# Two decode layers on one core: 256 rows of the second layer's w2 on a few partitions, in small loads among the large ones

## The chip, the cores and the metric

The kernel runs on one core of one Trainium2 chip. The metric is the device time of one execution in microseconds; lower is better. Every number below is from one profiled execution of the kernel before, or from its timed runs.

## The reference

Two layers, each an attention block and a gated feed-forward block, both with the same weights and the same caches, for four tokens in fp32:

```python
x = A_x                                           # 4 x 1 x 512
for _ in range(2):
    x = x + A(layernorm(x), k_cache, v_cache, wq, wo)
    x = x + B(layernorm(x), w1, w3, w2)

def A(x, k_cache, v_cache, wq, wo):               # 32 query heads, 8 KV heads, 4096 keys, 128 wide
    p = softmax(q @ k.T * 128 ** -0.5)
    return (p @ v) @ wo

def B(x, w1, w3, w2):                             # w1, w3: 512 x 1792, w2: 1792 x 512
    return (silu(x @ w1) * (x @ w3)) @ w2
```

## The kernel before

All weights and both caches come from HBM once per layer, except what is kept from layer 0 to layer 1 (wq, most of wo, and K and V of one head group, `TURN`). One buffer, `arena`, holds 216 units of 256 floats in each of 128 partitions. A list, `plan`, says in which order pieces are loaded; `pump` goes through it and issues each piece with one DMA on SyncE's queue (SP, L163) as soon as `take` finds room, and the instructions that read a piece call `done`, which gives its room back. On the chip SP works through its list strictly in order. Each DMA has one of eight semaphores, in turn, so a DMA is not issued before the one eight places ahead of it has landed; it also waits until TensorE (PE) has read what lay at its place.

In a layer, for each of eight head groups, PE forms the scores (`scores`, L371, into `s_ps`), VectorE (DVE) and ScalarE (ACT) the exponents, and PE the weighted sum of V (`weigh`, L414, into `o_ps`). `project_o` (L438, L445) multiplies by wo. Then comes `feed_forward`. w1 and w3 each come in two parts, "a" (columns 0 to 255 of each quarter of the 1792) and "b" (the other 192). `product` (L478) multiplies by them, into `s_ps` and `o_ps`; `gate` (ACT, L486, and DVE, L487) and `join` (DVE, L491) make h of them, with four tokens times four quarters on the partitions that are used. PE transposes h by 128 columns at a time (L525, L538, L540) and `tiles` (DVE, L494) copies the result to `hT`, 14 tiles of 128 x 4, which `down` multiplies with the 14 tiles of w2. In layer 1 a tile of w2 takes four matmuls (L503), one for each 128 columns of the output, each to its own 32 rows of `x_ps`; a matmul of fp32 is two instructions in the trace. `busy` (L259) issues matmuls whose result nobody reads. After the last tile DVE copies `x_ps` to `p` (L596) and SP stores it (L597).

In layer 1 the last loads are, in this order: 4 MB, 2 MB and 2 MB of V, w1a and w3a (2 MB each), w1b and w3b (1.5 MB each), and w2 in six loads of 1, 1, 0.5, 0.5, 0.25 and 0.25 MB. The first K of layer 0 comes in two loads of 4 MB, and the last V of layer 0 (group `TURN`) in four, of 4, 2, 1 and 1 MB, followed by wo.

Of the kernel before, what the change touches and what calls it, by code (L numbers as in the profile page):

```python
# [9 lines left out]
AF = mybir.ActivationFunctionType  # L10
# [4 lines left out]
LAYERS = 2  # L15
REP = HQ // HKV
P = 128
# [6 lines left out]
FA = 2 * P  # L24
FB = FJ - FA
WT = 14
EPS = 1e-5
SCALE = DH ** -0.5

# [5 lines left out]


@with_exitstack
def tile_decode_layers(ctx: ExitStack, tc: tile.TileContext, x, kt, v, wq, wo, w1, w3, w2, out):
# [51 lines left out]
    def cache(which, layer, g, parts, skip=0):  # L90
        src = (kt if which == "k" else v)[g]
        r = 8 * skip
        for n in parts:
            at = KEPT + r if (which, layer, g) in (("v", 0, TURN), ("k", 1, TURN - 2)) else None
            load(src[:, r * KB:(r + n) * KB], 8, [(which, layer, g, r // 8 + j) for j in range(n // 8)], at)
            r += n

    def weights(name, src, layer, parts, per, at=None, first=0):
        r = 0
        for n in parts:  # L100
            load(src[:, r * KB:(r + n) * KB], per, [(name, layer, first + r // per + j) for j in range(n // per)],
                 None if at is None else at + r)
            r += n
# [1 line left out]
    order = [list(range(HKV)), list(reversed(range(HKV)))]  # L105
    load(wq[:, 0:8 * KB], 8, [("wq", 0, 0)], WQ)
    for n in range(HKV):
        cache("k", 0, n, (32, 32) if n == 0 else (64,))
        if n == 0:
            load(wq[:, 8 * KB:64 * KB], 8, [("wq", 0, g) for g in range(1, HKV)], WQ + 8)  # L110
        else:
            cache("v", 0, n - 1, (64,))
    cache("v", 0, TURN, (32, 16, 8, 8))
    weights("wo", wo, 0, (32, 16, 8, 4, 4), 4, WO)

    def piece(name, i, at):
# [39 lines left out]
    def pump():  # L156
        while state["next"] < len(plan):
            src, per, keys, at = plan[state["next"]]
            n = src.shape[-1] // KB
            a = take(n, at)  # L160
# [69 lines left out]
    hT = qT.rearrange("p h c -> p (h c)")[:, 0:WT * B].rearrange("p (m b) -> p m b", b=B)  # L230
    top = const.tile([P, 32], F32, name="top")
    nc.vector.memset(top, 0.0)

# [236 lines left out]
    def feed_forward(layer, mean):  # L470
        keep = layer < LAYERS - 1
        h = p[:, 0:FJ]

        def product(name, ps, lo, n, fill=keep, ks=range(KC)):
            for k in ks:
                w = loaded(name, layer, k)
                for j in range(4):
                    nc.tensor.matmul(ps[32 * j:32 * j + 32, lo:lo + n], x32[:, k, :], w[:, j * n:(j + 1) * n],  # L478
                                     start=(k == 0), stop=(k == KC - 1))
                done(name, layer, k)  # L480
                if fill:
                    busy()

        def gate(lo, n):
            a = h[:, lo:lo + n]
            nc.scalar.activation(a, s_ps[:, lo:lo + n], AF.Sigmoid, scale=rstd)  # L486
            nc.vector.scalar_tensor_tensor(a, s_ps[:, lo:lo + n], rstd, a, op0=ALU.mult, op1=ALU.mult)  # L487

        def join(lo, n):
            a = h[:, lo:lo + n]  # L490
            nc.vector.scalar_tensor_tensor(a, o_ps[:, lo:lo + n], rstd, a, op0=ALU.mult, op1=ALU.mult)  # L491

        def tiles(lo, n):
            nc.vector.tensor_copy(hT[:, 4 * lo:4 * lo + n, :], t_ps.rearrange("p i (j b) -> p (i j) b", j=4)[:, 4 * lo:4 * lo + n, 0:B])  # L494

        def down(i):
            ws = [loaded("w2", layer, 2 * i + n) for n in range(2)]
            if keep:
                pair(i, lambda m: hT[:, m, :], lambda n: ws[n], i == 0, i == WT // 2 - 1)
            else:  # L500
                for n in range(2):
                    for k in range(KC):
                        nc.tensor.matmul(x_ps[32 * k:32 * k + B, 0:P], hT[:, 2 * i + n, :],  # L503
                                         ws[n][:, k * P:(k + 1) * P], start=False, stop=(i == WT // 2 - 1 and n == 1))
            for n in range(2):
                done("w2", layer, 2 * i + n)
            if keep and i < WT // 2 - 1:
                busy()
            elif not keep and i in (1, 3):
                busy(3)  # L510
# [12 lines left out]
        nc.scalar.activation(spare, half, AF.Exp)  # L523
        for i in range(2):
            nc.tensor.transpose(t_ps[:, i, :], h[:, i * P:(i + 1) * P], ident)  # L525
# [6 lines left out]
        if layer == LAYERS - 1:  # L532
            nc.vector.tensor_tensor(xt, xc, mu.unsqueeze(1).broadcast_to([P, KC, B]), op=ALU.add)
            for k in range(KC):
                nc.tensor.matmul(x_ps[32 * k:32 * k + B, 0:P], xt[:, k, :], ident, start=True, stop=False)

        def tail_tiles():
            nc.tensor.transpose(t_ps[:, 2, :], h[:, FA:FA + P], ident)  # L538
# [3 lines left out]
            tiles(2, 6)  # L542

        for i in range(1 if keep else 0, WT // 2):
            if i == (4 if keep else 0):
                tail_tiles()
            down(i)

    def run(pieces):
        for _ in pieces:  # L550
# [86 lines left out]
```

## Time and profile before

| | |
|---|---|
| timed runs | 708.88, 708.69 and 706.84 us, median 708.69 |
| the profiled execution's own time | 706.78 us |
| its span, first to last instruction | 705.0 us |
| HBM read | 298.85 MB |
| PE busy | 400.1 us (57%) |
| DVE busy, ACT busy | 85.0 us (12%), 38.3 us (5%) |
| SP's DMA queue | 99.1% of the time of the 16 DMA engines |

The share of a DMA queue is the time that its packets took, over 16 engines times the span; 99.1% means that hardly any engine was ever without a packet. A DMA is cut into packets, one for each row here, and spread over several of the 16 engines; each engine ends its part with a packet of 4 bytes that counts the semaphore up. The engine times are unions of the instructions' times. The time of an execution is 1.8 us more than its span.

### The profile page before, as it was taken

The numbers are of one execution on the slowest core, as the hardware profiler recorded it, in microseconds if no ns is written. First come the engines' busy times: TensorE is split into PE (matmuls) and PEld (weight loads), VectorE is DVE, ScalarE is ACT, GpSimd is POOL, SyncE is SP. The second block draws the span as 40 slices with busy tenths as digits, with TensorE's granted clock in tenths as the row PEclk, the third lists the DMA queues.
The fourth block names the chain that finished last, engine by engine and source line by source line (L and its number), as shares of the span: only waits on it lengthen the run. The fifth ranks groups of instructions, "written<-read, shape, count | busy, mean of one in ns | idle before, by whom it ended". The sixth has DMA issues, their size and how long they took to land. (4 is left out here: it accounts for less than half of the span.)

```text
span 705.0 us, 6895 instructions
## 1 busy us (share of the span) xinstructions
PE 400.1 (57%) x3082; PEld 132.1 (19%) x3082; DVE 85.0 (12%) x290; ACT 38.3 (5%) x87; POOL 2.9 (0%) x10
## 2 busy tenths in 40 slices
PE   4555454546555553547677894365563545467666
PEld 2111011111111120112143231011120111122224
DVE  2001010101011010101111111020010101010111
ACT  0000000000000000002001000000000000000101
POOL 0000000000000000000000000000000000000000
PEclk9766777777677787768899997587697878788899
DMA  9999999999999999999999999999999999999996
GB/s 387 461 403 472 414 417 436 450 417 431 455 416 432 435 436 420 442 421 423 413 404 406 416 438 438 446 424 421 461 421 424 440 439 421 431 432 419 426 425 270
DMA packets 14003, 299.35 MB, mean 425 GB/s; under 512 B 1687, under 2 KB 1815, under 8 KB 6551
## 3 DMA queue, kind: packets, MB, share of 16 engines
q1 hardware_dynamic: 13840, 298.92, 99.1%
q8 instruction: 24, 0.39, 0.2%
q10 hardware_dynamic: 135, 0.01, 0.0%
q14 instruction: 4, 0.03, 0.0%
HBM read 298.85 MB, written 0.07 MB: 424 GB/s over the span
## 5 line engine op out<-in xcount | busy, mean ns | idle before, releaser
L414 PE MATMUL o_ps<-arena 128*32 128x512 f32 x1024 | 145.7, 718 | 150.8 <-DMA arena<-in_v 137.6
L371 PE MATMUL s_ps<-arena,qpad 128*32 128x512 f32 x1024 | 152.1, 749 | 82.5 <-DMA arena<-in_kt 82.5
L414 PEld LDWEIGHTS o_ps<-arena 128*32 128x32 f32 x1024 | 37.3, 129 | 257.3 <-issue 224.5
L371 PEld LDWEIGHTS s_ps<-arena,qpad 128*32 128x32 f32 x1024 | 39.5, 133 | 177.7 <-issue 165.6
L423 DVE SCALAR_TENSOR_TENSOR p<-o_ps,parts,p 128x512 f32<-128x512 f32 x16 | 12.0, 750 | 270.9 <-PE o_ps L414 270.9
L378 DVE TENSOR_REDUCE top<-s_ps 128x1 f32<-128x512 f32 x16 | 11.0, 690 | 194.0 <-PE s_ps L371 194.0
L315 PE MATMUL o_ps<-arena,xpad 128*32 128x512 f32 x112 | 16.2, 707 | 10.5 <-DMA arena<-in_wq 10.5
L421 ACT ACTIVATE p<-o_ps,parts 128x512 f32<-128x512 f32 x16 | 11.0, 687 | 192.5 <-PE o_ps L414 184.6
L445 PE MATMUL x_ps<-arena,oT 128*4 128x512 f32 x104 | 14.1, 653 | 9.1 <-DMA arena<-in_wo 5.6
L402 PE MATMUL t_ps<-ident,p 128*128 128x128 f32 x64 | 11.2, 302 | 13.5 <-ACT p L396 13.5
L425 PE MATMUL t_ps<-ident,p 128*128 128x128 f32 x64 | 10.5, 287 | 14.3 <-DVE p L423 14.2
L389 ACT ACTIVATE f<-d 128x1 f32<-128x1 f32 x16 | 3.2, 203 | 256.3 <-DVE d L387 256.3
L396 ACT ACTIVATE p<-s_ps,top 128x512 f32<-128x512 f32 x16 | 10.9, 684 | 75.9 <-PE t_ps L425 75.9
L425 PEld LDWEIGHTS t_ps<-ident,p 128*128 128x128 f32 x64 | 6.7, 141 | 29.6 <-DVE p L423 29.6
L403 DVE COPY arena<-t_ps 128x512 f32<-128x512 f32 x16 | 11.1, 691 | 9.6 <-PE t_ps L402 9.6
L259 PE MATMUL m_ps<-ident,rows 128*32 128x128 f32 x70 | 11.9, 273 | 0.0
L402 PEld LDWEIGHTS t_ps<-ident,p 128*128 128x128 f32 x64 | 7.1, 147 | 22.2 <-ACT p L396 19.2
L478 PE MATMUL o_ps<-arena,xpad 128*32 128x192 f32 (+1 forms) x128 | 8.1, 360 | 2.9 <-DMA arena<-in_w 2.8
L478 PE MATMUL s_ps<-arena,xpad 128*32 128x192 f32 (+1 forms) x128 | 7.9, 359 | 2.3 <-DMA arena<-in_w 2.1
L259 PEld LDWEIGHTS m_ps<-ident,rows 128*32 128x32 f32 x70 | 7.5, 110 | 3.5
L315 PEld LDWEIGHTS o_ps<-arena,xpad 128*32 128x32 f32 x112 | 3.7, 126 | 20.7 <-DMA arena<-in_wq 11.6
L320 DVE COPY p<-o_ps 128x256 f32<-128x256 f32 x2 | 0.8, 424 | 44.9 <-PE o_ps L315 44.9
(97 smaller groups left out, 139.9 us busy)
## 6 DMA issues: line engine op xcount, KB each, us to landing
arena<-in_kt SPq DMA_DIRECT2D x4, 4096.0 KB, 20.1
arena<-in_v SPq DMA_DIRECT2D x4, 4096.0 KB, 33.0
arena<-in_w SPq DMA_DIRECT2D x17, 512.0 KB, 10.1
arena<-in_kt SPq DMA_DIRECT2D x8, 1024.0 KB, 9.8
arena<-in_wq SPq DMA_DIRECT2D x1, 7168.0 KB, 39.5
arena<-in_v SPq DMA_DIRECT2D x3, 2048.0 KB, 36.8
arena<-in_wo SPq DMA_DIRECT2D x1, 4096.0 KB, 25.5
arena<-in_kt SPq DMA_DIRECT2D x8, 512.0 KB, 8.2
```

Of the source, the lines that this page charges most:

```text
L259: nc.tensor.matmul(m_ps[turn["m"] ^ 1][0:32, 384:512], rows, ident, start=True, stop=True)
L315: nc.tensor.matmul(ps[32 * k:32 * k + 32, :], xpad[:, k, lo:lo + 32], w[:, k, :], start=first, stop=last)
L371: nc.tensor.matmul(s_ps[32 * b:32 * b + 32, :], qpad[:, b, lo:lo + 32], k[:, j, :], start=(blk == 0), stop=(blk == NB - 1))
L378: nc.vector.tensor_reduce(top[:, 0:1], s_ps, axis=AX.X, op=ALU.max, negate=True)
L402: nc.tensor.transpose(t_ps[:, i, :], p[:, i * P:(i + 1) * P], ident)
L403: nc.vector.tensor_copy(pT.rearrange("p i r -> p (i r)"), t_ps.rearrange("p i r -> p (i r)"))
L414: nc.tensor.matmul(o_ps[32 * b:32 * b + 32, :], pT[:, i, 32 * b:32 * b + 32], w[:, b, :], start=(i == 0), stop=(i == NI - 1))
L421: nc.scalar.activation(p, o_ps, AF.Copy, scale=st["parts"][:, 0:1])
L423: nc.vector.scalar_tensor_tensor(p, o_ps, st["parts"][:, 1:2], p, op0=ALU.mult, op1=ALU.add)
L425: nc.tensor.transpose(t_ps[:, j, :], p[:, j * P:(j + 1) * P], ident)
L445: nc.tensor.matmul(x_ps[r:r + B, :], left(2 * i + n), w(n), start=first, stop=False)
L478: nc.tensor.matmul(ps[32 * j:32 * j + 32, lo:lo + n], x32[:, k, :], w[:, j * n:(j + 1) * n], start=(k == 0), stop=(k == KC - 1))
```

## The change

The last V of layer 0 comes in two loads of 4 MB in place of four, and the first K in one load of 8 MB in place of two. In layer 1, tiles 0 and 4 of w2 (rows 0 to 255 of the 1792) are no longer loaded as 128 partitions. They come as nine blocks: eight of 28 rows on partitions 0 to 27, and one of 32 rows on partitions 0 to 31. The eight blocks lie side by side, 16 KB in a partition, and come in four loads, each of every fourth partition (7 rows of 16 KB); the ninth is a load of 32 rows of 2 KB. These five loads (`aside`) stand ahead of w1a, w3a, w1b, w3b and the first large load of w2. The other 12 tiles come in loads of 0.75, 0.75, 0.5, 0.5, 0.25 and 0.25 MB. For the nine blocks h has to be transposed in pieces of 28 (and 32) columns, by nine matmuls with the identity, and each block takes four matmuls with as many contraction rows (`few`). The residual's matmuls (`xt`) and some of the blocks' now stand ahead of w3b's product, `gate` of part b stands behind the transposes, and an exponential on one column that layer 1 had there (for the ACT table) is gone, as is `busy(4)` ahead of it; `busy(3)` twice is now `busy(2)` twice.

```diff
-        cache("k", 0, n, (32, 32) if n == 0 else (64,))
+        cache("k", 0, n, (64,))
...
-    cache("v", 0, TURN, (32, 16, 8, 8))
+    cache("v", 0, TURN, (32, 32))
...
+    side = iter([(w2s[i::4], slice(i, FEW, 4), 0) for i in range(4)] + [(w2b, slice(0, 32), 16)])
+    def aside():
+        plan.append((*next(side), None))
+    aside()
     for part, per, at in (("a", 4, 0), ("b", 3, 16)):
         for name, w in (("w1", w1), ("w3", w3)):
             weights(name + part, w[:, at * KB:(at + 4 * per) * KB], 1, (4 * per,), per)
-    weights("w2", w2, 1, (8, 8, 4, 4, 2, 2), 2)
+            aside()
+    for m, parts in ((1, (6,)), (5, (6,)), (8, (4, 4, 2, 2))):
+        weights("w2", w2[:, 2 * m * KB:], 1, parts, 2, None, m)
...
+                nc.sync.dma_start(arena[per, (a + keys) * KB:(a + keys + n) * KB], src)
...
+        def columns(rows, m, w, last=False):
+            for k in range(KC):
+                nc.tensor.matmul(x_ps[32 * k:32 * k + B, 0:P], hT[rows, m, :], w[rows, k * P:(k + 1) * P],
+                                 start=False, stop=last)
+        def few(lo, hi):
+            for u in range(lo, hi):
+                at = (where["few"] + 2 * u) * KB
+                columns(slice(0, FEW if u < 8 else 32), WT + u, arena[:, at:at + 2 * KB])
...
-        if not keep:
-            busy(4)
-        gate(FA, FB)
-        nc.scalar.activation(spare, half, AF.Exp)
+        if keep:
+            gate(FA, FB)
+            nc.scalar.activation(spare, half, AF.Exp)
         for i in range(2):
             nc.tensor.transpose(t_ps[:, i, :], h[:, i * P:(i + 1) * P], ident)
+        if not keep:
+            for u in range(9):
+                n = FEW if u < 8 else 32
+                nc.tensor.matmul(t_ps[0:n, 2, B * u:B * u + B], h[0:32, FEW * u:FEW * u + n], ident[0:32, 0:B],
+                                 start=True, stop=True)
         tiles(0, 8)
+        if not keep:
+            nc.vector.tensor_copy(hT[0:32, WT:WT + 9, :], t_ps[0:32, 2, 0:9 * B].rearrange("p (u b) -> p u b", b=B))
+            gate(FA, FB)
+            nc.vector.tensor_tensor(xt, xc, mu.unsqueeze(1).broadcast_to([P, KC, B]), op=ALU.add)
+            for k in range(KC):
+                nc.tensor.matmul(x_ps[32 * k:32 * k + B, 0:P], xt[:, k, :], ident, start=True, stop=False)
+            few(0, 4)
         product("w3b", o_ps, FA, FB, ks=range(0, 2))
...
         product("w3b", o_ps, FA, FB, ks=range(2, KC))
         join(FA, FB)
...
+        few(4, 7)
+        tail_tiles()
+        few(7, 9)
+        for m in (1, 2, 3, 5, 6, 7, *range(8, WT)):
+            columns(slice(0, P), m, loaded("w2", layer, m), m == WT - 1)
+            done("w2", layer, m)
+            if m in (3, 7):
+                busy(2)
```

The order of the instructions, first on SP at the end of layer 1. A row is line, operation, tile written and tensor read, and partitions times elements; `x2` is two of them in a row. Before:

```order
L163 DMA arena<-in_v 128x4096 x2
L163 DMA arena<-in_w 128x4096 x2
L163 DMA arena<-in_w 128x3072 x2
L163 DMA arena<-in_w 128x2048 x2
L163 DMA arena<-in_w 128x1024 x2
L163 DMA arena<-in_w 128x512 x2
L597 DMA out<-p 128x128
```

and now:

```order
L184 DMA arena<-in_v 128x4096 x2
L178 DMA arena<-in_w2s 7x4096
L184 DMA arena<-in_w 128x4096
L178 DMA arena<-in_w2s 7x4096
L184 DMA arena<-in_w 128x4096
L178 DMA arena<-in_w2s 7x4096
L184 DMA arena<-in_w 128x3072
L178 DMA arena<-in_w2s 7x4096
L184 DMA arena<-in_w 128x3072
L178 DMA arena<-in_w2b 32x512
L184 DMA arena<-in_w 128x1536 x2
```

Each small load now stands ahead of a large one, and the first two loads of w2 are a quarter smaller; the last four are as before.

On PE, from w1b's product (the 16 matmuls into `s_ps`) to the end. Before:

```order
L478 MATMUL s_ps<-arena,xpad 32x192 x16
L259 MATMUL m_ps_120<-ident,rows 32x128 x4
L525 MATMUL t_ps<-ident,p 128x128 x2
L478 MATMUL o_ps<-arena,xpad 32x192 x16
L535 MATMUL x_ps<-ident,xt 4x128 x4
L538 MATMUL t_ps<-ident,p 128x128
L540 MATMUL t_ps<-ident,p 64x64 x2
L503 MATMUL x_ps<-arena,qT 4x128 x16
L259 MATMUL m_ps_120<-ident,rows 32x128 x3
L503 MATMUL x_ps<-arena,qT 4x128 x16
L259 MATMUL m_ps_120<-ident,rows 32x128 x3
L503 MATMUL x_ps<-arena,qT 4x128 x24
```

and now (`qT` is the memory in which `hT` lies):

```order
L499 MATMUL s_ps<-arena,xpad 32x192 x16
L548 MATMUL t_ps<-ident,p 128x128 x2
L552 MATMUL t_ps<-ident,p 28x4 x8
L552 MATMUL t_ps<-ident,p 32x4
L560 MATMUL x_ps<-ident,xt 4x128 x4
L528 MATMUL x_ps<-arena,qT 4x128 x16
L499 MATMUL o_ps<-arena,xpad 32x192 x16
L528 MATMUL x_ps<-arena,qT 4x128 x12
L569 MATMUL t_ps<-ident,p 128x128
L571 MATMUL t_ps<-ident,p 64x64 x2
L528 MATMUL x_ps<-arena,qT 4x128 x20
L280 MATMUL m_ps_119<-ident,rows 32x128 x2
```

Behind the last row come 12 matmuls into `x_ps`, two more of `busy` and 24 into `x_ps`. Between w1b's product and w3b's stand 31 matmuls where there were six.

More of the change, by code (lines that the diff above doesn't have):

```diff
@@ L26 @@
 WT = 14
+FEW = 28
 EPS = 1e-5
@@ L37, in tile_decode_layers @@
 @with_exitstack
-def tile_decode_layers(ctx: ExitStack, tc: tile.TileContext, x, kt, v, wq, wo, w1, w3, w2, out):
+def tile_decode_layers(ctx: ExitStack, tc: tile.TileContext, x, kt, v, wq, wo, w1, w3, w2, w2s, w2b, out):
     nc = tc.nc
@@ L159, in pump @@
             n = src.shape[-1] // KB
+            if isinstance(per, slice):
+                where.setdefault("few", None if "few" in where else take(18))
+                a = where["few"]
+                if a is None:
+                    del where["few"]
+                    return
+                nc.sync.dma_start(arena[per, (a + keys) * KB:(a + keys + n) * KB], src)
+                state["next"] += 1
+                continue
             a = take(n, at)
@@ L229, in tile_decode_layers @@
     oT = const.tile([P, HKV, REP, B], F32, name="oT")
-    hT = qT.rearrange("p h c -> p (h c)")[:, 0:WT * B].rearrange("p (m b) -> p m b", b=B)
+    hT = qT.rearrange("p h c -> p (h c)")[:, 0:(WT + 9) * B].rearrange("p (m b) -> p m b", b=B)
     top = const.tile([P, 32], F32, name="top")
@@ L493, in tiles @@
         def tiles(lo, n):
-            nc.vector.tensor_copy(hT[:, 4 * lo:4 * lo + n, :], t_ps.rearrange("p i (j b) -> p (i j) b", j=4)[:, 4 * lo:4 * lo + n, 0:B])
+            slots = t_ps.rearrange("p i (j b) -> p (i j) b", j=4)
+            nc.vector.tensor_copy(hT[:, lo:lo + n, :], slots[:, lo:lo + n, 0:B])
         def down(i):
             ws = [loaded("w2", layer, 2 * i + n) for n in range(2)]
[L498 to L504, printed above, removed]
+            pair(i, lambda m: hT[:, m, :], lambda n: ws[n], i == 0, i == WT // 2 - 1)
             for n in range(2):
                 done("w2", layer, 2 * i + n)
-            if keep and i < WT // 2 - 1:
+            if i < WT // 2 - 1:
                 busy()
-            elif not keep and i in (1, 3):
-                busy(3)
+        def columns(rows, m, w, last=False):
[6 more added lines that the diff above has]
+                columns(slice(0, FEW if u < 8 else 32), WT + u, arena[:, at:at + 2 * KB])
         sq = squares()
@@ L531, in feed_forward @@
         join(FA, FB)
[L532 to L535, printed above, removed]
         def tail_tiles():
@@ L541, in tail_tiles @@
                                  start=True, stop=True)
[L542 to L547, printed above, removed]
+            tiles(8, 6)
+        if keep:
+            for i in range(1, WT // 2):
+                if i == 4:
+                    tail_tiles()
+                down(i)
+            return
+        few(4, 7)
+        tail_tiles()
+        few(7, 9)
[4 more added lines that the diff above has]
+                busy(2)
     def run(pieces):
@@ L626 @@
         "w2": lay(np.concatenate([full, rest], axis=1)).reshape(P, WT * D),
+        "w2s": lay(w2j[0, :8 * FEW].reshape(8, FEW, D).transpose(1, 0, 2)).reshape(FEW, 8 * D),
+        "w2b": lay(w2j[0, 8 * FEW:2 * P]),
     }
```

## The prediction

> **What bounds the kernel now.** I read the page first, for what is busy, then the chain that ended last, then the end in windows of half a microsecond. The page, with the 40 slices of the DMA engines' busy share and the queues:
>
> ```profile
> span 705.0 us, 6895 instructions
> DMA  9999999999999999999999999999999999999996
> q1 hardware_dynamic: 13840, 298.92, 99.1%
> q8 instruction: 24, 0.39, 0.2%
> q10 hardware_dynamic: 135, 0.01, 0.0%
> ```
>
> The loads' queue fills 16 engines for 99.1% of the span, and only the last slice is below nine tenths. So time is won or lost only through bytes, their rate, their spread over the engines, or the work behind the last byte. q8 fetches instructions: 24 packets of 16 KB take 0.2% x 16 x 705 = 22.6 us of engine time, 0.94 us each, on whichever engines serve it. The end of the chain (start, length, what):
>
> ```profile
> 643.63 41.49 DMA arena<-in_w
> ...
> 685.19 16.14 DMA arena<-in_w
> 701.33 0.04 issue
> 701.37 0.45 PE x_ps L503 x8
> ...
> 701.84 0.29 DVE p L596
> ```
>
> The last load lands at 701.33 us, one tile's matmuls and a copy follow. Everything that ends the kernel is on this line: landing, then 0.49 us to the end of PE's work, then 3.2 us for the copy and the store to 705.0. Now the end by windows; the last two columns are the share of 16 DMA engines and GB/s:
>
> ```profile
> 696.00:697.00 1.00, 1.00 (x30) 0.95 (x18) 0.00 (x0) 0.00 (x0) 0.00 (x0) 1.00 0.88 344
> 697.00:697.50 0.50, 0.22 (x3) 0.00 (x0) 0.00 (x0) 0.00 (x0) 0.00 (x0) 1.00 0.70 279
> 697.50:698.00 0.50, 0.45 (x18) 0.44 (x22) 0.00 (x0) 0.00 (x0) 0.00 (x0) 1.00 0.68 270
> 698.00:698.50 0.50, 0.50 (x25) 0.49 (x14) 0.00 (x0) 0.00 (x0) 0.00 (x0) 1.00 0.52 209
> 698.50:699.00 0.50, 0.50 (x13) 0.50 (x12) 0.00 (x0) 0.00 (x0) 0.00 (x0) 1.00 0.49 197
> 699.00:699.50 0.50, 0.50 (x19) 0.34 (x10) 0.00 (x0) 0.00 (x0) 0.00 (x0) 1.00 0.42 168
> 700.00:700.50 0.50, 0.42 (x16) 0.33 (x16) 0.00 (x0) 0.00 (x0) 0.00 (x0) 1.00 0.43 164
> ```
>
> 0.70 of 16 is 11 engines, 0.49 is 8, 0.42 is 7: nine engines end between 696.5 and 699.5, and seven go on alone to about 701. Each engine got the same bytes of the loads, so something else held the seven up; the fetches of q8, by their size, are the likely one, though no view names the engine of a packet.
>
> **The loads, part by part.** How many engines a load uses follows from the packet counts above. 96 loads and stores of 128 rows at 128 + 16 packets, and one of 8 rows at 8 + 8, make 13840; the ACT queue's 120 rows make 135 = 120 + 15. So 128, 8 and 120 rows ran on 16, 8 and 15 engines, each the largest number up to 16 that divides the rows. Then 7 rows run on seven engines and 32 on 16. The rate of one engine, from the stretch of large loads and from the middle of the tail:
>
> ```profile
> 200.00:300.00 100.00, 53.18 (x370) 16.21 (x366) 10.80 (x33) 4.80 (x11) 0.00 (x0) 0.76 1.00 434
> 320.00:340.00 20.00, 14.53 (x110) 4.57 (x110) 3.47 (x9) 3.30 (x6) 0.00 (x0) 0.91 0.99 419
> 360.00:370.00 10.00, 7.41 (x93) 3.78 (x93) 1.37 (x6) 0.59 (x2) 0.56 (x1) 1.00 1.03 400
> 692.00:693.00 1.00, 0.45 (x12) 0.39 (x16) 0.00 (x0) 0.44 (x2) 0.00 (x0) 1.00 1.02 414
> ```
>
> 434 / 16 = 27.1 GB/s for long rows, 414 / 16 = 25.9 at the end. Every engine loses two tiles of w2, 32 KB, and gains 4 KB of the ninth block: 28 KB / 25.9 = 1.11 us less. Seven engines get four rows of 16 KB more: 64 KB / 27.1 = 2.42, so 1.31 us more in all. Whether the landing moves down or up hangs on which seven. If they are among the nine early ones, the late seven land 1.11 us earlier, and the loaded ones at the latest at 699.5 + 1.3 = 700.8. If they are the late seven, the landing moves up by 1.31. No row tells engines apart. [...]
>
> Layer 0's last V: 4 MB in rows of 16 and 8 KB become rows of 32 KB. Between 419 GB/s (the stretch in which they land) and 434 lie 4.19 MB / 419 - 4.19 MB / 434 = 0.35 us; nothing is the other end. I take 0.2 us for all engines. The first K's rows go from 32 to 64 KB: nothing to see.
>
> What the two joined loads cost: PE can start only when all has landed. For V:
>
> ```profile
> 334.34 3.64 PE L414 MATMUL o_ps<-arena 128*32 128x512 f32 x32 [1.21 <-ACT p L421]
> 345.17 6.82 PE L445 MATMUL x_ps<-arena,oT 128*4 128x512 f32 x48 [5.59 <-DMA arena<-in_wo]
> ```
>
> The second half's 32 instructions end at 337.98 and PE then waits 5.59 us for wo. The four last blocks would start at most 3.64 us later; the wait for wo covers that. I cost it at nothing; without that cover it would be up to 3.6 us on all that follows. The first K behaves alike: half of its scores come later, while loads issued long before keep coming. SP's five more loads, against three fewer before, shift who waits for which of the eight semaphores: the last load of w2 will wait for the fourth small one instead of w3a. Behind that one stand 4.3 MB up to the last load, 10 us at 419 GB/s, more than the spread of the engines, so none runs dry.
>
> [...]
>
> **PE behind w1b, part by part.** The added matmuls lie beside loads only as long as PE keeps ahead of the landings. The rows of the tail:
>
> ```profile
> 682.45 1.11 PE L297 MATMUL m_ps<-rows,p 128*128 128x4 f32 x8 [0.56 <-DVE p L290]
> 684.06 1.45 PEld L478 LDWEIGHTS s_ps<-arena,xpad 128*32 128x32 f32 x32 [0.36 <-DVE xpad L301]
> 688.95 1.51 PE L478 MATMUL s_ps<-arena,xpad 128*32 128x192 f32 x32 [0.56 <-DMA arena<-in_w]
> 690.97 0.42 DVE L487 SCALAR_TENSOR_TENSOR p<-s_ps,rstd,p 128x192 f32<-128x192 f32 x1 [1.93 <-ACT p L486]
> 691.22 0.44 PE L525 MATMUL t_ps<-ident,p 128*128 128x128 f32 x2
> 691.69 0.19 DVE L494 COPY qT<-t_ps 128x32 f32<-128x32 f32 x1 [0.31 <-PE t_ps L525]
> 692.55 1.51 PE L478 MATMUL o_ps<-arena,xpad 128*32 128x192 f32 x32 [0.89 <-DMA arena<-in_w]
> 694.12 0.42 DVE L491 SCALAR_TENSOR_TENSOR p<-o_ps,rstd,p 128x192 f32<-128x192 f32 x1 [2.24 <-PE o_ps L478]
> 694.46 0.17 DVE L533 TENSOR_TENSOR xt<-xpad,mu 128x16 f32<-128x16 f32 x1
> 694.68 0.40 PE L535 MATMUL x_ps<-ident,xt 128*4 128x128 f32 x8 [0.62 <-DVE xt L533]
> 695.01 0.33 PE L538 MATMUL t_ps<-ident,p 128*128 128x128 f32 x1
> 695.53 1.06 PE L503 MATMUL x_ps<-arena,qT 128*4 128x128 f32 x32
> 696.40 0.82 PE L259 MATMUL m_ps<-ident,rows 128*32 128x128 f32 x6
> ```
>
> Now PE waits for loads (0.89 us before w3b, for instance). The new order, from w1b's start at 688.95 - 0.2 = 688.75: product 1.51, two transposes 0.44, to 690.7. Nine small transposes are 18 instructions; they load 28 columns of weights and stream four. No row shows that: 1.45 / 32 = 0.045 us each (weights of 32 columns) is one end, 0.8 us in all, and 1.11 / 8 = 0.139 (128 columns, four streamed) the other, 2.5 us. The first is nearer, since loading sets the pace in both; with some for four streamed columns I take 0.06, 1.1 us: 691.8. DVE, in its order: copy 0.19, gate 0.42, xt 0.17, with 0.1 between them: 692.7. PE: xt's matmuls 0.33 to the next, four blocks at the price of four tiles 1.06, w3b 1.51: 695.6. join 0.48 with its start, beside three blocks (0.80): 696.4. Tail transposes 0.52 (695.01 to 695.53), two blocks 0.53, three tiles 0.80, `busy(2)` 0.45 (two thirds of 0.82, part of it overlapped), three tiles 0.80, `busy(2)` 0.45, six tiles 1.59: 701.5. With the ends of the small transposes: 701.2 and 702.9.
>
> **The sum.** The end of PE's work was 701.82. By the loads it would be 701.33 - 1.11 - 0.2 + 0.49 = 700.5, up to 701.1 if a loaded engine is last. By PE it is 701.5. The later one holds: 0.3 us less, 706.78 - 0.3 = 706.5 us against this execution's own time. That execution was 1.9 us below the median of the runs (708.69; one run at 706.84, two at 708.7 to 708.9), a spread as large as all I argue about; 0.3 below the median is 708.4. I state the middle of the two, 707.4 us.
>
> **The rivals.** (a) PE keeps up, and the loads set the end: shorter transposes, or blocks that run faster with 28 rows. Then 1.3 us less, 705.5 or 707.4 by the median. For it speaks that my PE chain is a sum of separate rows; against it that it holds hardly a wait to shorten. (b) Slower: the seven engines of the small loads are the late seven. It decides as soon as one loaded engine ends later than 700.0: landing 701.33 + 1.31 - 0.2 = 702.4, 1.1 us more, 707.9 or 709.8. [...] (c) Slower: the small transposes cost their upper end and PE ends at 702.9, 1.1 us more. (d) The load of 7 rows runs on one engine: 28 rows of 16 KB / 27.1 are 16.9 us on it, less 1.1; even the earliest engine, done at 696.5, would then end near 712, 11 us more, 718. The packet counts speak against. (e) The joined V or K opens a gap, or the runs' two levels change their mix: 2 us either way, 704.7 or 710.7.
>
> **How the numbers follow.** Forecast 0.40, (a) 0.27, (b) 0.11, (c) 0.08, (d) 0.02, (e) 0.12, evenly both ways. A measurement here can hardly tell 0.3%, 2.1 us, from no change. Forecast, (a), (b) and (c) all lie inside it; a twentieth of them, half to each sign, I give to the levels of the runs, and with (e) and (d) that makes faster 0.08, same 0.82, slower 0.10. The range goes from (a) on the low level, 705.5, with half a microsecond for its terms, 705.0, to (b) by the median, 709.8; it leaves out (d), (e) and little more.
>
> **What will show it.** In q1, 13512 packets: 93 x 144 for 128 rows, 16 for x, 4 x 14 and 48 for the small loads; a count under 13500 would mean fewer than seven engines. In the windows of the end, a steeper fall of the share, with no stretch of seven engines alone; a longer stretch at seven means (b). On PE, w3b's product not waiting for its load and starting near 694.1, the small transposes near 1.1 us, and the last tiles' matmuls back to back; if PE waits for the last load of w2, it is (a). Around 338 to 345 us PE must still wait for wo. The prediction is wrong if the time moves by more than 2.1 us, which none of these terms gives but (d) and (e).

## The result, and the profile after

The changed kernel takes 710.91 us (median of 16 runs, 708.01 to 714.51) where the kernel before takes 707.25 on the same chip (16 runs, 706.69 to 708.88): ratio 1.0053, 95% interval 1.0038 to 1.0068. It is slower by 3.7 us, and its runs lie three times as far apart. The profiled execution took 709.30 us, with a span of 706.4.

The queues on the page after:

```profile
q1 hardware_dynamic: 13512, 298.92, 99.0%
q8 instruction: 24, 0.39, 0.2%
```

The packets are the 13512 that were worked out, so seven rows did run on seven engines. The end of the chain that ended last (start, length, what):

```profile
683.37 3.64 PE s_ps L499 x32
...
687.95 3.57 PE o_ps L499 x32
691.53 1.78 PE s_ps L499 x32
...
693.67 0.62 PE t_ps L552 x18
...
696.44 1.44 PE o_ps L499 x32
...
701.99 1.37 PE x_ps L528 x44
703.39 0.29 DVE p L637
```

Before, this chain ended with a load and 0.45 us of PE. Now no load is on it from 683 us to the end of PE's work at 703.36, 1.5 us later than before, and PE's products of w1a and w3a take 3.64 and 3.57 us where those of w1b and w3b later take 1.78 and 1.44 (w1b's and w3b's are a quarter smaller). The windows show why; the last three columns are the granted clock, the share of 16 DMA engines, and GB/s:

```profile
682.00:692.00 10.00, 9.74 (x86) 5.31 (x90) 1.73 (x9) 0.47 (x1) 0.55 (x1) 0.51 1.00 415
700.00:700.50 0.50, 0.50 (x22) 0.49 (x11) 0.00 (x0) 0.00 (x0) 0.00 (x0) 1.00 0.23 90
701.50:702.00 0.50, 0.50 (x19) 0.47 (x18) 0.00 (x0) 0.00 (x0) 0.00 (x0) 1.00 0.13 49
702.00:702.50 0.50, 0.50 (x29) 0.43 (x22) 0.00 (x0) 0.00 (x0) 0.00 (x0) 1.00 0.05 20
```

For ten microseconds PE ran at half clock. And the loads end later too: at 700.0 to 700.5 us, where seven engines were at work before, fewer than four are (0.23 x 16), but two go on (0.13 x 16) until about 702.2. PE's rows of the end, and around wo:

```profile
345.06 8.28 PE L466 MATMUL x_ps<-arena,oT 128*4 128x512 f32 x48 [4.40 <-DMA arena<-in_wo]
...
691.30 2.01 PE L499 MATMUL s_ps<-arena,xpad 128*32 128x192 f32 x32
693.24 0.44 PE L548 MATMUL t_ps<-ident,p 128*128 128x128 f32 x2
693.61 0.67 PE L552 MATMUL t_ps<-ident,p 32*28 32x4 f32 x18
...
696.37 1.51 PE L499 MATMUL o_ps<-arena,xpad 128*32 128x192 f32 x32
```

From w1b's product to the end of PE's work lie 703.36 - 691.30 = 12.06 us without a wait for a load. Two things are then to be explained: that this chain starts 2.35 us later than w1b's product did before (688.95), and that it ends the kernel.

### The profile page after: what moved, and what is told of

Same layout as the page of the kernel before. It is cut to its first block, busy times and chain, and to the rows that moved or that the text cites. A ratio compares the mean times of both kernels' runs of the same rounds, so it can differ in the third digit from the quotient of the medians.

```text
span 706.4 us, 7023 instructions
## 1 busy us (share of the span) xinstructions
PE 407.4 (58%) x3144; PEld 136.7 (19%) x3144; DVE 85.1 (12%) x291; ACT 36.8 (5%) x85; POOL 2.9 (0%) x10
## 3 DMA queue, kind: packets, MB, share of 16 engines
q1 hardware_dynamic: 13512, 298.92, 99.0%
## 5 line engine op out<-in xcount | busy, mean ns | idle before, releaser
L435 PE MATMUL o_ps<-arena 128*32 128x512 f32 x1024 | 149.9, 735 | 150.4 <-DMA arena<-in_v 137.8
L392 PE MATMUL s_ps<-arena,qpad 128*32 128x512 f32 x1024 | 149.4, 739 | 85.0 <-DMA arena<-in_kt 85.0
L466 PE MATMUL x_ps<-arena,oT 128*4 128x512 f32 x104 | 15.6, 717 | 7.9 <-DMA arena<-in_wo 4.4
L499 PE MATMUL s_ps<-arena,xpad 128*32 128x192 f32 (+1 forms) x128 | 10.1, 441 | 1.8 <-DMA arena<-in_w 1.5
L499 PE MATMUL o_ps<-arena,xpad 128*32 128x192 f32 (+1 forms) x128 | 9.8, 423 | 1.9 <-DMA arena<-in_w 1.8
```

What stands on the lines that cost most here:

```text
L392: nc.tensor.matmul(s_ps[32 * b:32 * b + 32, :], qpad[:, b, lo:lo + 32], k[:, j, :], start=(blk == 0), stop=(blk == NB - 1))
L435: nc.tensor.matmul(o_ps[32 * b:32 * b + 32, :], pT[:, i, 32 * b:32 * b + 32], w[:, b, :], start=(i == 0), stop=(i == NI - 1))
L466: nc.tensor.matmul(x_ps[r:r + B, :], left(2 * i + n), w(n), start=first, stop=False)
```

## The experiments

All are timed against the kernel before on the same chip; "over before" is the difference of the two medians, and "kept warm" means that PE's waits from 671 us on are filled with matmuls whose result nobody reads.

| kernel | us | over before | ratio, 95% interval |
|---|---|---|---|
| changed kernel | 710.91 | +3.66 | 1.0053 (1.0038 to 1.0068) |
| before, K and V joined | 706.62 | -0.55 | 0.9994 (0.9984 to 1.0003) |
| changed, K and V not joined | 710.27 | +3.10 | 1.0046 (1.0026 to 1.0067) |
| changed loads alone | 708.53 | +1.36 | 1.0017 (1.0008 to 1.0025) |
| changed tail of PE alone | 706.76 | -0.41 | 0.9998 (0.9985 to 1.0011) |
| changed, PE kept warm | 708.21 | +1.26 | 1.0020 (1.0010 to 1.0031) |
| tail of PE alone, kept warm | 706.54 | -0.41 | 0.9992 (0.9983 to 1.0000) |
| before, joined, kept warm | 706.53 | -0.44 | 0.9992 (0.9983 to 1.0001) |
| changed, small loads behind w1b | 709.82 | +2.87 | 1.0034 (1.0021 to 1.0048) |
| the same, kept warm | 709.01 | +2.04 | 1.0030 (1.0015 to 1.0045) |
| warm, no loads of 28 rows | 705.65 | -1.28 | 0.9980 (0.9971 to 0.9988) |
| warm, no load of 32 rows | 707.89 | +0.96 | 1.0013 (1.0004 to 1.0022) |
| four loads of 32 rows, 16 engines (not warm) | 712.80 | +5.85 | 1.0078 (1.0061 to 1.0094) |
| warm, two loads of 14 rows | 712.74 | +5.77 | 1.0087 (1.0068 to 1.0105) |
| the same, rows farther apart in HBM | 712.29 | +5.25 | 1.0070 (1.0053 to 1.0086) |
| warm, four loads of 16 rows | 711.67 | +4.70 | 1.0074 (1.0050 to 1.0098) |
| the same, to every eighth partition | 710.80 | +3.87 | 1.0052 (1.0040 to 1.0065) |
| warm, four loads of 8 rows, every fourth partition | 707.63 | +0.59 | 1.0013 (0.9996 to 1.0029) |
| warm, four loads of 8 neighbouring rows | 715.52 | +8.41 | 1.0120 (1.0103 to 1.0137) |

### The parts alone

The joined K and V loads by themselves, in the kernel before:

```diff
-        cache("k", 0, n, (32, 32) if n == 0 else (64,))
+        cache("k", 0, n, (64,))
-    cache("v", 0, TURN, (32, 16, 8, 8))
+    cache("v", 0, TURN, (32, 32))
```

> The kernel before with only the joined loads: the first K of layer 0 in one load, the last V in two. Theory L (the small loads stand on engines that also fetch instructions, so the last byte lands later) and theory P (PE's added work behind w1b ends the kernel): no loss, 0 to 0.3 us less, ratio 0.999 to 1.000. Theory J (the joined loads open a gap or delay PE in layer 0): most of the 3.7 us, ratio 1.003 to 1.006.

They cost nothing: 0.9994. The profile of this run also shows, by chance, what half clock does to the old order. Its window, and PE's rows from w1b on:

```profile
682.00:692.00 10.00, 9.73 (x91) 5.09 (x94) 1.81 (x8) 0.47 (x1) 0.55 (x1) 0.50 0.99 419
```

```profile
687.27 3.64 PE L478 MATMUL o_ps<-arena,xpad 128*32 128x256 f32 x32
690.69 2.10 PE L478 MATMUL s_ps<-arena,xpad 128*32 128x192 f32 x32
...
693.95 1.51 PE L478 MATMUL o_ps<-arena,xpad 128*32 128x192 f32 x32
```

and the last PE step of its chain:

```profile
700.15 1.51 PE x_ps L503 x45
```

The same ten microseconds at half clock, and w1b's product also late, at 690.69; yet PE was done at 701.66 in this execution of 706.53 us. Behind w1b the old order needs 10.97 us, and in the profile of before it had 12.87 (688.95 to 701.82), the rest being waits for loads. That rest, 1.9 us, takes up a late start. The new order took 12.06 with half a microsecond of half clock in it, and takes 11.50 at full clock (693.59 to 705.09 in the run of PE's tail alone, below). Of the 12.87 us that leaves 1.4 us of rest, and the start was 2.35 us late.

The changed kernel with the old K and V loads:

```diff
-        cache("k", 0, n, (64,))
+        cache("k", 0, n, (32, 32) if n == 0 else (64,))
-    cache("v", 0, TURN, (32, 32))
+    cache("v", 0, TURN, (32, 16, 8, 8))
```

> The changed kernel with the old K and V loads: only the 256 rows of w2 are changed. Theories L and P: ratio 1.004 to 1.006, as the whole change. Theory J: 0.999 to 1.001.

The loss is all here. In its profile the clock was full until w1b, so the loads are seen better than in the changed kernel's own:

```profile
690.65 1.51 PE L499 MATMUL s_ps<-arena,xpad 128*32 128x192 f32 x32 [2.30 <-DMA arena<-in_w]
...
695.46 2.77 PE L499 MATMUL o_ps<-arena,xpad 128*32 128x192 f32 x32 [0.16 <-DMA arena<-in_w]
```

w1b's product waits 2.30 us for its load and starts 1.7 us later than before; w3b's starts 2.9 us later and takes 2.77 us in place of 1.51. Its windows around w3b:

```profile
695.40:695.60 0.20, 0.14 (x4) 0.14 (x8) 0.00 (x0) 0.00 (x0) 0.00 (x0) 0.83 1.04 430
695.60:698.80 3.20, 3.20 (x48) 1.75 (x48) 0.42 (x1) 0.00 (x0) 0.00 (x0) 0.50 0.94 372
698.80:699.00 0.20, 0.20 (x12) 0.13 (x8) 0.00 (x0) 0.00 (x0) 0.00 (x0) 0.64 0.83 328
```

Half clock from about 695.5 to 698.9, 3.4 us; the wait of 2.30 us had ended 4.9 us before, and the longest wait of PE here from 668 us on was 2.48 us, at 675.76. What brought half clock on is not shown.

Loads as changed with PE's old tail (tiles 0 and 4 take the weights of tiles 1 and 5), and PE's new tail with the old loads (the blocks read what lies in w1a's place):

```diff
 # loads alone
+ws = [loaded("w2", layer, 2 * i + n + (not keep and 2 * i + n in (0, 4))) for n in range(2)]
 # PE's tail alone
-                at = (where["few"] + 2 * u) * KB
+                at = (where["w1a", layer, 0][0] + 2 * (u % 8)) * KB
```

> The loads of w2 as changed (small ones too), but PE's work behind w1b as before: tiles 0 and 4 are multiplied with the weights of tiles 1 and 5 and the small loads are never read, so the result lacks them. Old K and V loads. Theory L: 2 to 4 us slower (1.003 to 1.006), the last load landing 1 us or more later than 701.3 and PE ending 0.5 us behind it. Theory P: within 0.7 us of before, since the last bytes land about when they did.

> PE's work as changed, but all loads as before, all 14 tiles of w2 in 128 rows: the blocks' matmuls read w1a's place instead of their weights, and tiles 0 and 4 are loaded and not read. Old K and V loads. Theory L: within 0.7 us of before, the last load landing near 701.3 and PE not far behind it. Theory P: 2 to 4 us slower (1.003 to 1.006), with PE ending 1.5 us or more behind the last landing.

Neither gives the loss: +1.36 and -0.41, where both together give +3.1 to +3.7. So it isn't a sum of the parts; late loads and the longer chain meet. In the loads alone, PE waits for the last load until 703.26, 1.9 us later than before (701.37):

```profile
703.26 0.40 PE L524 MATMUL x_ps<-arena,qT 128*4 128x128 f32 x8 [0.23 <-DMA arena<-in_w]
```

Ten of the twelve runs of PE's tail alone lie at 706.3 to 707.2, one at 709.55, and the profiled one at 710.99. Its rows:

```profile
690.17 3.62 PE L496 MATMUL o_ps<-arena,xpad 128*32 128x256 f32 x32
693.59 1.51 PE L496 MATMUL s_ps<-arena,xpad 128*32 128x192 f32 x32
...
703.51 1.58 PE L525 MATMUL x_ps<-arena,qT 128*4 128x128 f32 x45
```

w1b's product starts 4.6 us late, behind products at half clock, though the loads were on time. Two causes were left: the clock and the loads' lateness.

### The clock

The filling matmuls (`busy`):

```diff
+                if layer and g == 0 and NI * f + i in (3, 5, 7):
+                    busy({3: 5, 5: 12, 7: 5}[NI * f + i])   # weigh, last V
+        if layer and g == 0:
+            busy(3)                                         # before wo
+            busy(3)                                         # behind wo
+            busy(2)                                         # before w3a
+            busy(4)                                         # before w1b
+            busy(4)                                         # behind the transposes
```

> The changed kernel, with matmuls whose result nobody reads put into PE's waits from 671 us on (5, 12 and 5 around the last V's, 3 and 3 around wo's, 2 and 4 around w3a's product, 4 before the copies of the transposes), so that the granted clock should stay at 1.0. Theory C (half of the loss is the clock: PE's chain from the last V on has no slack left for the products at half clock): products at 1.93 us instead of 3.64, w1b's product starts when w1b lands, 690.3, PE ends near 702.5, time 708.5 as with the changed loads alone, runs close together. Theory L (only the late landing of w1b and of the last load counts): 710.9 as changed, since the landings are the same.

> Loads as before, the tail of PE as changed (as in the run of PE's tail alone), with the same filling matmuls as in the warm run. Theory C: the runs at 709.6 and 711.0 of PE's tail alone came from the clock, so all runs lie between 706.2 and 707.3. Theory L: the filling does nothing, median 706.8 with a run in six near 710.

> The kernel before with the joined K and V loads and the same filling matmuls, as a version that may beat both. Its end hangs on the last load's landing, 701.3, and its order of PE's work leaves room for products at half clock, so theory C gives it next to nothing: 706.5, ratio 0.999, with the upper runs near 708.7 gone. A ratio under 0.997 would mean that the clock also costs the kernel before.

The changed kernel falls from +3.66 to +1.26 over before, and nine of its twelve runs lie within 0.8 us (707.87 to 708.64). Where the loads are as before the filling changes next to nothing (-0.41 both times with the new tail, but its highest run is now 707.90 and not 710.99; -0.55 and -0.44 with the old one). So about 2.4 us of the loss are the granted clock, and in the median they are lost only with the changed loads. The warm kernel's rows:

```profile
686.09 1.93 PE L503 MATMUL o_ps<-arena,xpad 128*32 128x256 f32 x32 [0.21 <-DMA arena<-in_w]
...
690.48 1.51 PE L503 MATMUL s_ps<-arena,xpad 128*32 128x192 f32 x32 [1.61 <-DMA arena<-in_w]
```

w3a's product takes 1.93 us, and w1b's now waits for its load, which comes 1.5 us later than before. The profiled execution is one of the other three, 709.57 us; at its end half clock came back:

```profile
701.00:701.50 0.50, 0.50 (x16) 0.28 (x9) 0.00 (x0) 0.00 (x0) 0.00 (x0) 0.50 0.27 90
```

In the changed kernel the filling makes half clock rarer (the granted clock, in the mean of the executions, is 0.807 in place of 0.799); it doesn't exclude it.

### The late loads

The four loads of 28 rows moved behind w1b, cold and warm:

```diff
-    aside()
     for part, per, at in (("a", 4, 0), ("b", 3, 16)):
...
-            aside()
+            if part == "b":
+                for _ in range({"w1": 4, "w3": 1}[name]):
+                    aside()
```

> The changed kernel, with the four loads of 28 rows between w1b and w3b and not ahead of w1a, w3a, w1b and w3b; the fifth stays behind w3b. Theory W (w1b comes late on the loaded engines, and PE's chain starts there): w1b lands near 688.9 again and w3b as in the changed kernel, 695.1; up to 1.4 us less, 709.5 to 710. Theory C (clock): w1b isn't what PE waits for when the products run at half clock; 710.9 and the same spread. Theory B (last byte alone): the same bytes per engine, 710.9.

> The changed kernel with both: the four loads of 28 rows between w1b and w3b, and the matmuls that fill PE's waits. If the late w1b and the clock are two separate costs that add (1.1 us and 2.7 us alone), 707.1; if they are the same loss reached in two ways, 708.2 as the warm kernel, since the last load's landing is the same (702.2).

Cold it is 0.8 us better than the changed kernel, with intervals that overlap; warm it is no better than the warm kernel. Rows of the warm one:

```profile
688.71 1.51 PE L504 MATMUL s_ps<-arena,xpad 128*32 128x192 f32 x32 [0.42 <-DMA arena<-in_w]
...
695.10 1.51 PE L504 MATMUL o_ps<-arena,xpad 128*32 128x192 f32 x32 [1.73 <-DMA arena<-in_w]
...
704.31 0.61 PE L533 MATMUL x_ps<-arena,qT 128*4 128x128 f32 x8 [1.79 <-DMA arena<-in_w]
```

w1b is on time again, but w3b is as late as ever, and PE waits there instead. Where the small loads stand among the large ones matters little (708.21 us ahead, 709.01 behind w1b, both kept warm); without the four it is 705.65, as shown next. The last row is discussed further down.

Then each kind of small load was left out of the warm kernel:

```diff
 # no loads of 28 rows
+                if keys == 16:
                     nc.sync.dma_start(arena[per, (a + keys) * KB:(a + keys + n) * KB], src)
 # no load of 32 rows
+                if keys != 16:
                     nc.sync.dma_start(arena[per, (a + keys) * KB:(a + keys + n) * KB], src)
```

> The warm kernel without its four loads of 28 rows: the eight blocks are multiplied with what lies at their place (so the output isn't the reference's), every engine has 32 KB less than before and 4 KB of the ninth block more. Theory L (what the warm kernel has left over the kernel before is the four loads): w1b lands at 688.8 and w3b at 692.5 as before, the last load near 700.3, and PE's chain from w1b ends near 701; 705.7 to 706.3. Theory P (PE's longer chain costs by itself): 707.5 or more.

> The warm kernel without the load of 32 rows by 2 KB (the ninth block is multiplied with what lies at its place). By its bytes, 4 KB on each engine, it costs 0.15 us: 708.0. If a load of few rows on all 16 engines slows the others' packets, as the even loads did (+3.5 to +4.5 us for 0.44 to 0.5 MB), it costs up to 0.6 us: 707.6. More than 1 us would make it the main cost of the loads.

Without the four loads the time falls by 2.5 us, to 1.28 below before. Rows of it:

```profile
688.79 1.51 PE L504 MATMUL s_ps<-arena,xpad 128*32 128x192 f32 x32 [0.52 <-DMA arena<-in_w]
...
693.40 1.51 PE L504 MATMUL o_ps<-arena,xpad 128*32 128x192 f32 x32
...
699.49 1.57 PE L533 MATMUL x_ps<-arena,qT 128*4 128x128 f32 x45
```

```profile
699.00:700.00 1.00, 1.00 (x34) 0.93 (x28) 0.00 (x0) 0.00 (x0) 0.00 (x0) 1.00 0.45 158
700.00:700.50 0.50, 0.50 (x25) 0.43 (x19) 0.00 (x0) 0.00 (x0) 0.00 (x0) 1.00 0.00 0
```

w1b is on time, w3b waits for nothing, and the loads end before 700. So PE's longer chain by itself costs nothing over the kernel before; the theory that it does falls. But PE and not the loads ends this kernel, at 701.06. Without the load of 32 rows the time falls by 0.3 us, and the intervals overlap, so the times can't tell its cost from nothing.

### Spread evenly

If seven engines with 64 KB more are the trouble, the same bytes on more engines should cure it. Eight blocks of 32 rows in four loads of 32 rows by 4 KB; the warm kernel with two loads of 14 rows; with four of 16 rows by 8 KB:

```diff
-    side = iter([(w2s[i::4], slice(i, FEW, 4), 0) for i in range(4)] + [(w2b, slice(0, 32), 16)])
 # 32 rows (FEW = 32, no w2b)
+    side = iter([(w2s[:, 4 * i * KB:4 * (i + 1) * KB], slice(0, FEW), 4 * i) for i in range(4)])
 # 14 rows
+    side = iter([(w2s[i::2], slice(i, FEW, 2), 0) for i in range(2)] + [(w2b, slice(0, 32), 16)])
 # 16 rows (FEW = 32, no w2b)
+    side = iter([(w2s[i::2, 8 * j * KB:8 * (j + 1) * KB], slice(i, FEW, 2), 8 * j) for j in range(2) for i in range(2)])
```

> The tail of PE as changed, but tiles 0 and 4 come as eight blocks of 32 rows in four loads of 32 rows by 4 KB, on all 16 DMA engines alike, ahead of w1a, w3a, w1b and w3b (K and V loads as before). Every engine gets the bytes it had before. Theory E (the seven loaded engines): the last landing returns to 701.3, w1b's landing to 688.8, and the time to that of PE's tail alone, 706.8, with a single run in some at 709 to 711. Theory S (small loads cost as such, whatever engines they use, or the blocks' place ahead of w1a): 710 to 711 as changed.

> The warm kernel (708.2), but the eight blocks of 28 rows come in two loads of 14 rows by 16 KB, one ahead of w1a and one ahead of w1b, so that 14 engines take 32 KB more each instead of seven 64 KB. Theory E (the 1.7 us between the warm kernel and PE's warm tail with the loads as before are the seven loaded engines): w1b lands near 689, the last load near 701.4, 706.6 to 707. Theory S (loads of few rows cost as such): 708.2 as the warm kernel, perhaps 0.5 less for two loads fewer.

> The warm kernel, but with eight blocks of 32 rows in four loads of 16 rows by 8 KB, one row on each of the 16 engines. The loads of 32 rows by 4 KB, also even, gave 712.8, with the engines' rate at 300 to 390 GB/s from 672 to 696 us. Theory E: all engines carry what they did before, the rate stays near 420, 706.5 to 707. Theory R (a small load on all 16 engines slows the others' packets, whatever its rows): the rate falls as with 32 rows, 709 or more even with the clock kept up.

All three are much slower, and my theory of the seven engines, as I had put it, failed its test. The window from 672 to 696 us, in the order before, 32 rows, 14 rows, 16 rows:

```profile
672.00:696.00 24.00, 16.70 (x229) 9.03 (x225) 4.80 (x19) 2.85 (x6) 0.55 (x1) 0.93 1.00 420
```

```profile
672.00:696.00 24.00, 16.34 (x130) 7.06 (x130) 3.53 (x14) 0.95 (x3) 0.55 (x1) 0.72 1.01 352
```

```profile
672.00:696.00 24.00, 17.60 (x180) 11.37 (x172) 3.52 (x14) 0.95 (x3) 0.55 (x1) 0.93 0.99 334
```

```profile
672.00:696.00 24.00, 19.63 (x218) 12.80 (x211) 3.52 (x14) 1.33 (x4) 0.55 (x1) 0.93 1.00 349
```

The engines are as busy as ever (1.00 of 16) and move 334 to 352 GB/s in place of 420: half a megabyte of small rows slows 10 MB of large ones around it. Three things could do that: where the rows lie in HBM, the number of engines, or the partitions that they write.

```diff
 # 14 rows, twice as far apart in HBM (w2s laid out twice side by side)
+    side = iter([(w2s[i::2, 0:16 * KB], slice(i, FEW, 2), 0) for i in range(2)] + [(w2b, slice(0, 32), 16)])
 # 16 rows, to partitions 0, 8, ... 120
+    side = iter([(w2s[i::2, 8 * j * KB:8 * (j + 1) * KB], slice(i, P, 8), 8 * j) for j in range(2) for i in range(2)])
 # 8 rows, every fourth
+    side = iter([(w2s[i::4], slice(i, FEW, 4), 0) for i in range(4)])
 # 8 neighbouring rows
+    side = iter([(w2s[8 * i:8 * i + 8], slice(8 * i, 8 * i + 8), 0) for i in range(4)])
```

> The kernel of two loads of 14 rows by 16 KB (712.7), with the rows twice as far apart in HBM, so that the rows of one load lie 64 KB apart as in the loads of seven rows (there 32 KB). Theory H (rows near each other in HBM slow the other reads): the rate returns to about 420 GB/s from 672 to 696 us, 707 to 708. Theory M (it hangs on how many engines a small load uses, not on where it reads): 336 GB/s again, 712.7.

> The kernel of four loads of 16 rows by 8 KB (711.7), but the rows go to every eighth partition (0, 8, ... 120) in place of every second of 0 to 31, so that each engine writes where its rows of the large loads lie too, if rows are dealt out in order. The blocks are multiplied with what then lies on partitions 0 to 31, so the output isn't the reference's; PE's work is the same. Theory O (the large packets slow down because all engines write to few partitions): the rate stays near 420 GB/s from 672 to 696 us, 706.5 to 707.5. Theory R (a small row on all engines does it wherever it goes): 323 to 369 GB/s again, 711.7.

> The warm kernel with eight blocks of 32 rows in four loads of 8 rows by 16 KB on eight engines, and no ninth block (64 KB more on eight engines in place of seven, no load on all 16). By bytes alone as the warm kernel without its last load, 707.9. Theory M: if the slowdown grows with the engines used, one more engine shows little, 708 to 709; if it sets in as soon as the rows are a divisor of 16 (8, 16 and 32 rows against 7), 711 to 712, but then 14 rows would not have shown it.

> The kernel of four loads of 8 rows by 16 KB (707.6), but each load takes eight neighbouring rows to eight neighbouring partitions (0 to 7, 8 to 15, ...) in place of every fourth; the same data at the same place in the end, the same eight engines and bytes. Theory M (it hangs on the number of engines): 707.6 again, 420 GB/s from 672 to 696 us. [...]

Twice the distance in HBM doesn't cure it (712.29, 352 GB/s), and spreading the rows over all partitions doesn't cure it (710.80, 362 GB/s). Eight engines with every fourth partition show no slowdown; eight engines again (13472 packets in both), with the same bytes and final places but neighbouring rows in a load, show the longest time of all. Their windows, every fourth first (that profile is of the slowest of its ten executions, 713.14 us, with half clock from 692 to 705.8; the rate is full all the same):

```profile
672.00:696.00 24.00, 21.65 (x249) 15.10 (x242) 4.21 (x18) 1.37 (x4) 0.55 (x1) 0.92 1.00 420
```

```profile
672.00:696.00 24.00, 17.51 (x174) 11.50 (x169) 3.52 (x14) 0.95 (x3) 0.55 (x1) 0.86 1.00 343
```

Two things differ between these two, 7.9 us between the medians: the partitions that a load's rows go to, and how far apart the rows lie in HBM (64 KB with every fourth row, 16 KB with neighbours). As rows 64 KB apart were slow with fourteen rows, the partitions are the likely cause; no run changes them alone with eight rows. Over all cases, rows 4 partitions apart kept the rate (420 GB/s), and rows 2 apart (334, 349 and, farther apart in HBM, 352), 8 apart (362) and 1 apart (343 in loads of eight rows, 352 in four of 32) didn't. No row shows which partitions an engine writes or what an engine waits for, so why rows 4 apart were quick is not shown. The changed kernel's four loads go to every fourth partition like the quick ones. Its load of 32 rows on 16 engines slows the others a little: from 672 to 696 us the seven kernels that have it and no slower small loads move 411 to 415 GB/s, and the seven with neither 419 to 422.

No version that multiplies all its weights beats the kernel before by more than the measurement tells; the lowest is before with joined loads, kept warm or not (706.53 and 706.62).

## Why the prediction was wrong

**Loads or PE, "the later one holds".** This step failed first. It took w1b's landing 0.2 us earlier than before, and so let PE's chain start at 688.75. But three small loads stand ahead of w1b and four ahead of w3b. If the same seven engines take them all, that is 48 and 64 KB on each, at my own 27.1 GB/s 1.8 and 2.4 us. The rows agree: w1b's product starts 1.5 to 1.7 us later where it waits for its load, w3b's 2.6. I worked out the loads only for the last landing, where 28 KB fewer had already been saved; ahead of w1b nothing had been.

**The seven loaded engines.** I took them to be among the early nine and gave the other case, rival (b), 0.11. In kind it is what happens with PE's old tail: the loads alone, in which PE waits for the last load until 703.26, take 1.36 us more than before, and rival (b)'s sum is -1.11 - 0.2 + 2.42 = +1.1. But the expected stretch of seven late engines isn't there; two are late, and no row tells whether they are loaded ones. In the changed kernel PE doesn't wait for that load. That the four loads fall on the same seven engines each time, on which the 64 KB and the 2.42 us rest, no run shows. What the runs show in its place is that the time falls by 2.54 us without the four loads; that this is so close to 2.42 is in part luck, since PE ends that kernel.

**The clock.** This is the larger failure: it stood in none of my terms, put at nothing without a reason. My rows of PE were all at full clock; the profile of before has half clock at 676 to 679 us, and I took that for one execution's accident. It is one, but one that the old order absorbed and the new one with the changed loads can't: 2.4 us, and the spread of the runs. With the clock kept up the changed kernel takes 708.21, inside the range. The range ended at 709.8 with rival (b) and left out rival (e), which I had thought of as a shift of 2 us either way; neither is a chain losing its slack.

**The base.** I started from the median of three runs, 708.69, and one execution of 706.78. Sixteen runs give 707.25, so the forecast of 707.4 stands for no change.

**The sum by the runs.** Before with joined loads and warm -0.44; 28 KB less on each engine, with the new tail and the load of 32 rows, -0.84 (from -0.44 to -1.28; I had 1.11); the four loads +2.54; the clock +2.40. Together +3.66, as each term is the step from one kernel of the table to the next. The differences are of medians of different sessions, each good to some 0.5 us.

**What held.** The joined loads cost nothing, and PE still waits 4.40 us for wo. The number of engines. PE's chain from w1b on, 12.06 us (0.5 of it half clock) where I had 12.75 (688.75 to 701.5), with the last tiles back to back. The small transposes took 0.67 us, below my lower end of 0.8, so rival (c) was none; 18 instructions at 0.037 us are cheaper than their weight loads' rows let expect (with four columns streamed in both, 28 columns of weights took 0.037 us and 128 took 0.139). Rival (d) falls with the packet count. Rival (a) would need PE to wait for the last load, which it doesn't. w3b's product started at 696.37, not 694.1: the first sign, in the list of what to look for, of what was missing. Pricing small loads by bytes, for which the window of before at 360 to 370 us spoke (loads of 0.375 and 0.5 MB, a share of 1.03, 400 GB/s), was right for the four (420 GB/s from 672 to 696 us in the run with eight rows, as before), but by luck: I hadn't thought of the partitions that they go to. The four cost 2.54 us together.

## What to carry to other kernels

When bytes are moved to some of the DMA engines, follow the lateness to every load that stands behind them in the queue and that someone waits for, not just to the last; an order of work that has filled its waits absorbs less of a late load or a half clock (here it had 1.4 us of waits left in place of 1.9), so price the slack you use up. Try more than one choice of partitions for a load of few rows: here every fourth of 0 to 31, on seven or eight engines, left the loads around it at 411 to 420 GB/s, and the other choices brought them down to 334 to 362. Try a suspected clock loss by filling the waits with idle matmuls: here it took the changed kernel from 710.91 to 708.21 us.

## What the runs showed of the hardware that was not expected

Half a megabyte in loads of eight rows cost nothing in rate with one choice of rows (420 GB/s, 707.63 us) and 7.9 us with another (343 GB/s, 715.52 us), at the same number of engines, bytes and final places.

Half clock came in whole multiples of 3.41 us: from 668 us to the end of PE's work, 3.41 (before; K and V not joined; the warm kernel), 6.82 (8 neighbouring rows), 10.24 (changed; before, joined), 13.65 (loads alone; 8 rows, every fourth) and 17.07 (PE's tail alone). The length of a wait of PE doesn't settle when it comes. Behind waits of 2.9 us it began after 0.4 to 1.2 us (before, loads alone, PE's tail alone); behind one of 2.02 us after 1.2 (8 rows, every fourth), behind 2.01 and 2.21 after some 6.6 (before, joined; changed), and behind 2.48 not for 19 us (K and V not joined). At the end of this kernel it costs 2.4 us, as much as the four loads.

In the warm kernel with the small loads behind w1b, one engine ended the kernel alone. The last tile's row above waits 1.79 us, and the window and the queues of that time are:

```profile
702.50:703.00 0.50, 0.01 (x2) 0.00 (x0) 0.00 (x0) 0.00 (x0) 0.00 (x0) 1.00 0.03 4
```

```profile
q1 hardware_dynamic: 29, 0.05, 5.7%
q8 instruction: 1, 0.02, 2.2%
```

From 701 to 704 us the loads' queue has 29 packets left, and one instruction fetch of 16 KB lies among them; 2.2% of 16 engines for 3 us are 1.06 us. The trace has it from 701.79 to 702.83. While it runs, the last engine's packets stand still, as no packet of any queue starts here:

```profile
701.95:702.80 0.85, 0.53 (x15) 0.11 (x8) 0.00 (x0) 0.00 (x0) 0.00 (x0) 1.00 0.00 0
```

The loads' next packet starts at 702.82, so the fetch did hold that engine up. The four packets behind it took 0.21 to 0.23 us where those ahead took 0.08 to 0.09. Which engines fetched in the other executions stays open.
